# Cross attention and a max-out layer on one core: the state transposes go to the DMA queue, and GpSimd and VectorE work is reordered

## The chip, the cores and the metric

One core of one Trainium2 chip runs the whole kernel. The metric is the device time of one execution in microseconds; the time before is 148.46 us, the median of three runs (148.19 to 148.90).

## The reference

There are eight batches (B = 8) with eight heads (H = 8). Each head has 512 rows of x and 32 rows of state, 64 numbers wide.

```python
a = softmax(x @ state.T / 8)          # 512 x 32 for each batch and head
xread = a @ state                     # 512 x 64
a2 = softmax(state @ x.T / 8)         # 32 x 512
sread = a2 @ x                        # 32 x 64
attn = concatenate([xread, sread], axis=rows)      # 544 rows a batch
y = attn, heads laid side by side, (8*544) x 512
out = maximum(y @ w1, y @ w2) @ w_out              # 512 -> 1024 -> 512
```

## The kernel before

The kernel never forms xread. With wd = w1 - w2 it uses max(h1, h2) = relu(y wd) + y w2, so a batch's output is relu(A (S wd)) w_out + A (S (w2 w_out)), where A holds the softmax rows and S the state. For each batch it needs these pieces:

- `xt`, the batch's x transposed, and `sbd`, the transposed states in block form, for the scores. `scores_mm` and `scores_ev` make `e`, the exponentials. `reduce_pair` or `norm_sums` sum them and take the reciprocal (`er`), and `norm_mul` multiplies them to `a` (A, bf16).
- `aT`, `a` transposed: for batches 0 and 1 by TensorE (`at_mm`, eight transposes into two PSUM banks, copied out by `at_ev`), for later batches by a DMA (`at_dma`).
- `sw`, the state times wd, and the state times wwo = w2 w_out (`sw_mm`, `sw_two_mm`, `sw_h_mm`; copies `sw_ev`).
- first layer `l1_mm` (L426) with its relu `l1_ev` into `r`; second layer `l2_open` (L438) and `l2_f` (L442), copied to `ob` by `l2_out` and stored.
- `sread` for the state rows (`sread_mm`, `sread_norm`, `sread_tr_mm`), finished for all batches at the end (`moe_sread`).

The order of the instructions on every engine is the order in which the source issues them; no scheduler moves them. PSUM has two pools of four banks, `ps` and `pa` (tile names `ps` and `acc` in the profile). All loads, stores and DMA transposes go through SP's queue in source order, except for the first state load. An instruction that waits holds up everything behind it on its engine.

The opening stage, up to about 36 us, prepares the weights while batch 0 and then batch 1 run through it. Weights come in as f32 quarters of 512 KB and are cast to bf16 (`w2_cast`, `wo_cast`; the first quarter in halves: `w2_cast_h`, `w1_cast_h`, `wo_cast_h`); `w_sub` makes a quarter of wd; `w2_tr_mm` transposes a quarter of w2; `w_wo_mm` and `w_wo_h_mm` multiply it with w_out, and `w_wo_ev` adds up the rounds. `idle` issues matmuls on zeros while TensorE would wait. The states of batches 2 to 7 are loaded (`load_states`), cast on GpSimd (`states_cast`), transposed by TensorE (`states_mm`, line 157) into one bank, and copied to `sbd` by two engines (`states_ev`). For batch 2 on, x is cast by GpSimd in two halves (`cast_half`, `cast_x`) and transposed by a DMA (`xt_dma`); `cast_xo` makes another cast copy. A function `states_dma`, which transposes the states by a DMA into a buffer of the pool that holds the x casts, is in the source of the kernel before but not called.

After the opening, a loop over batches 1 to 7 issues one batch's second layer between the next batch's scores and first layer.

Of the kernel before, what the change touches and what calls it, by code (L numbers as in the profile page):

```python
# [15 lines left out]
def kernel(  # L16
# [9 lines left out]
    nc = tc.nc  # L26
    B, H, S, D = x.shape
    _, _, Ns, _ = state.shape
# [3 lines left out]
    NC = S // 128  # L32
# [14 lines left out]
    pa = ctx.enter_context(tc.tile_pool(name="pa", bufs=4, space=bass.MemoryType.PSUM))  # L47
    ctx.enter_context(tc.manual_schedule())

    def bank(dtype=F32, pool=None):  # L50
        n = 512 if dtype == F32 else 1024
        if pool is pa:
            return pa.tile([128, n], dtype, tag="acc", name="acc")
        return ps.tile([128, n], dtype, tag="ps", name="ps")

    def copy(eng, o, i):
        if eng == "A":
            nc.scalar.copy(o, i)  # L58
        elif eng == "V":
            nc.vector.tensor_copy(o, i)  # L60
        else:
            nc.gpsimd.tensor_copy(o, i)  # L62
# [20 lines left out]
    xf_t, st = {}, {}  # L83
# [40 lines left out]
    P = {}  # L124
# [26 lines left out]
    def states_cast(eng):  # L151
        copy(eng, sbr.rearrange("p m j d -> p j m d"), sfr.rearrange("p j (m d) -> p j m d", m=8))

    def states_mm(pool=None):
        p = P["st"] = bank(BF16, pool)
        for m in range(8):
            nc.tensor.transpose(p[:, m * 128:(m + 1) * 128], sbr[:, m].rearrange("p j d -> p (j d)"), ident)

    def states_dma():
        P["st"] = xio.tile([128, NC * 256], BF16, tag="xb", name="stt")  # L160
        nc.sync.dma_start_transpose(out=P["st"].rearrange("p (m r) -> p m r", m=8), in_=sbr.rearrange("p m j d -> p (m j d)"))

    def states_ev(j, eng):
        o = sbd[64 * j:64 * j + 64, 2:B, :, 32 * j:32 * j + 32].rearrange("p b k (l m) -> p (b k) l m", l=4)
        copy(eng, o, P["st"][64 * j:64 * j + 64, :].rearrange("p (m k l) -> p k l m", m=8, l=4)[:, 8:])


    def cast_half(b, g, eng):
        if b not in st:
            st[b] = dict(xb=xio.tile([128, NC, H * D], BF16, tag="xb", name="xb"))  # L170
        copy(eng, st[b]["xb"][:, :, 256 * g:256 * g + 256].rearrange("p c (i d) -> p i c d", i=4),
             xf_t[b][:, 4 * g:4 * g + 4, :].rearrange("p i (c d) -> p i c d", c=NC))
# [39 lines left out]
    def scores_pair_mm(b, k, pool):  # L212
        d = st[b]
        if "e" not in d:
            att_tiles(b)
        p = P["sc", k] = bank(F32, pool)
        for c in range(NC):
            nc.tensor.matmul(p[:, c * 64:c * 64 + 64], d["xt"][:, c, k, :], sbd[:, b, k, :],
                             start=(c == 0), stop=(c == NC - 1))

    def scores_pair_ev(b, k):
        nc.scalar.activation(out=st[b]["e"][:, :, :, k, :].rearrange("p g c n -> p c g n"),
                             in_=P["sc", k][:, 0:256].rearrange("p (c g n) -> p c g n", c=NC, g=2), func=ACTF.Exp, scale=scale)
# [6 lines left out]
    def xt_dma(b):  # L230
        d = st[b]
        d["xt"] = at.tile([128, NC, 4, 128], BF16, tag="xt", name="xt")
        nc.sync.dma_start_transpose(out=d["xt"].rearrange("p c k t -> p (c k) t"),
                                    in_=d["xb"].rearrange("p c m -> p (c m)"))
# [39 lines left out]
    def scores_ev(b, hh):  # L274
        ev = st[b]["e"].rearrange("p g c i n -> p (g c) i n")[:, :, 2 * hh:2 * hh + 2, :]
        nc.scalar.activation(out=ev.rearrange("p (g c) i n -> p g c (i n)", g=2),  # L276
                             in_=P["sc", hh].rearrange("p (c g m) -> p g c m", c=NC, g=2), func=ACTF.Exp, scale=scale)
# [5 lines left out]
    def norm_sums(b, hh, sums=True):  # L283
        d = st[b]
        if sums:
            ev = d["e"].rearrange("p g c i n -> p (g c) i n")[:, :, 2 * hh:2 * hh + 2, :]
            nc.vector.tensor_reduce(d["es"][:, hh], ev, axis=mybir.AxisListType.X, op=ALU.add)  # L287
        nc.vector.reciprocal(d["er"][:, hh], d["es"][:, hh])

    def norm_mul(b, hh, eng):  # L290
        d = st[b]
        ev = d["e"].rearrange("p g c i n -> p (g c) i n")[:, :, 2 * hh:2 * hh + 2, :]
        av = d["a"].rearrange("p g c i n -> p (g c) i n")[:, :, 2 * hh:2 * hh + 2, :]
        (nc.gpsimd if eng == "P" else nc.vector).tensor_mul(  # L294
            av, ev, d["er"][:, hh].unsqueeze(3).to_broadcast([128, 2 * NC, 2, Ns]))

    def norm(b, hh, eng, sums=True):
        norm_sums(b, hh, sums)
        norm_mul(b, hh, eng)
# [12 lines left out]
    def at_mm(b, g, pool=None):  # L312
        if b not in AT:
            AT[b] = keep.tile([128, 2, NC, 128], BF16, tag="at", name="aT")
        p = P["at", g] = bank(BF16, pool)
        for c in range(NC):
            nc.tensor.transpose(p[:, c * 128:(c + 1) * 128], st[b]["a"][:, g, c].rearrange("p i n -> p (i n)"), ident)

    def at_ev(b, g, eng):
        copy(eng, AT[b][:, g].rearrange("p c t -> p (c t)"), P["at", g][:, 0:512])  # L320
# [43 lines left out]
    def sw_ev(b, lo, hi, g, eng):  # L364
        copy(eng, SW[b][:, g, lo:hi], P["sw", b, lo][g][:, 0:hi - lo])
# [53 lines left out]
    R, OB, ACC = {}, {}, [None] * NC  # L419
# [16 lines left out]
    def l2_open(b, c, p, start, stop):  # L436
        for g in range(2):
            nc.tensor.matmul(p, AT[b][:, g, c, :], SW[b][:, g, FF:WC], start=(start and g == 0), stop=(stop and g == 1))  # L438

    def l2_f(b, c, p, fs, start, stop):  # L440
        for j, f in enumerate(fs):
            nc.tensor.matmul(p, R[b][:, f, c * 128:(c + 1) * 128], wo[:, f, :],  # L442
                             start=(start and j == 0), stop=(stop and j == len(fs) - 1))

    def l2_out(b, c, p, eng):
        if b not in OB:
            OB[b] = big.tile([128, NC, DM], F32, tag="ob", name="ob")
        copy(eng, OB[b][:, c, :], p)
# [62 lines left out]
    def w1_cast_h(j, eng):  # L511
        copy(eng, w1b[:, :, 128 * j:128 * j + 128], w1f[0][:, :, 128 * j:128 * j + 128])

    def wo_cast_h(j, eng):
        copy(eng, wo[:, j, :], wof[0][:, j, :])

    def w2_tr_h_mm(j, pool=None):
        p = P["w2h", j] = bank(BF16, pool)
        for i in range(4):
            nc.tensor.transpose(p[:, i * 128:(i + 1) * 128], w2b[0][:, i, j * 128:(j + 1) * 128], ident)  # L520

    def w2_tr_h_ev(j, eng):
        copy(eng, w2t[:, j].rearrange("p i t -> p (i t)"), P["w2h", j][:, 0:512])
# [15 lines left out]
    def w_sub(q, i0, i1, eng):  # L539
        (nc.gpsimd if eng == "P" else nc.vector).tensor_sub(  # L540
            wd[:, i0:i1, q * FQ:(q + 1) * FQ], w1f[q][:, i0:i1], w2f[q][:, i0:i1])
# [12 lines left out]
    def w_wo_h_mm(i, j, pool=None):  # L554
        if j == 0:
            P["wwo", 0, i] = bank(F32, pool)
        nc.tensor.matmul(P["wwo", 0, i], w2t[:, j, i, :], wo[:, j, :], start=(j == 0), stop=(j == 1))
# [16 lines left out]
    def l2_part(q, c):  # L574
        if ACC[c] is None:
            ACC[c] = bank(F32, pa)
        l2_f(0, c, ACC[c], (2 * q, 2 * q + 1), q == 0, False)
# [67 lines left out]
    xt_pair_ev(0, 3, "A")  # L645
    idle(1)
    scores_pair_mm(0, 2, None)
    wo_cast_h(0, "P")
    scores_pair_ev(0, 2)
    reduce_pair(0, 2)  # L650
    idle(5)
    scores_pair_mm(0, 3, pa)
    scores_pair_ev(0, 3)
    w2_tr_h_mm(0)
    w1_cast_h(1, "P")
    w1_cast_h(0, "A")
    idle(3)
    sread_mm(0, pa)
# [1 line left out]
    sw_h_mm(0, pa)  # L660
    reduce_pair(0, 3)
    norm_sums(0, 1, False)
    norm_mul(0, 1, "V")
    w2_tr_h_ev(0, "A")
    sw_ev(0, 0, 128, 1, "A")
    idle(4)
    w_wo_h_mm(1, 0)
    at_mm(0, 0, pa)
    sw_ev(0, 0, 128, 0, "A")
    at_mm(0, 1)  # L670
    w_sub(0, 0, 4, "P")
    w_wo_h_mm(3, 0)
    w2_cast_h(1, "A")
    at_ev(0, 1, "V")
    sw_h_mm(1, pa)
    sw_ev(0, 128, 256, 1, "V")
    wo_cast_h(1, "P")
    w2_tr_h_mm(1)
    at_ev(0, 0, "A")
    l1_mm(0, 0)  # L680
# [103 lines left out]
    scores_mm(1, 1)  # L784
    l2_part(2, 2)
    states_cast("P")
    scores_ev(1, 0)
    cast_half(2, 0, "P")
    scores_ev(1, 1)
# [3 lines left out]
    sw_ev(0, FF, WC, 0, "A")  # L793
    norm_sums(1, 0)
    norm_mul(1, 0, "P")
    l2_part(3, 2)
    l2_part(3, 1)
    l2_part(3, 3)
    sw_mm(1, FF, WC)
    norm_sums(1, 1)  # L800
    sw_ev(1, FF, WC, 0, "A")
    sread_mm(1)
    norm_mul(1, 1, "P")
    l2_open(0, 3, ACC[3], False, True)
    l2_open(0, 2, ACC[2], False, True)
    l2_out(0, 3, ACC[3], "A")
# [1 line left out]
    at_ev(1, 0, "A")  # L808
    sw_ev(1, FF, WC, 1, "V")
    at_mm(1, 1)  # L810
    cast_half(2, 1, "P")
    sread_norm(1)
    states_mm()
    states_ev(1, "A")
    at_ev(1, 1, "V")
    cast_xo(2)
    l2_out(0, 2, ACC[2], "V")
    l2_open(0, 0, ACC[0], False, True)
    l2_open(0, 1, ACC[1], False, True)
    states_ev(0, "V")  # L820
    l2_out(0, 1, ACC[1], "A")
    l2_out(0, 0, ACC[0], "V")
    l1_mm(1, 6, pa)
    cast_half(3, 1, "P")
    l1_ev(1, 6, "A")
# [4 lines left out]
    l1_mm(1, 7)  # L830
    l1_mm(1, 1, pa)
    l1_mm(1, 3, pa)
    xt_dma(2)
    l1_ev(1, 5, "A")
    l1_ev(1, 0, "V")
    l1_mm(1, 2)
# [13 lines left out]
    for b in range(1, B):  # L850
        n = b + 1
# [65 lines left out]
```

## Time and profile before

| | |
|---|---|
| median of the runs | 148.46 us |
| the profiled execution's own time | 148.07 us |
| its span, first to last instruction | 146.3 us |
| TensorE busy | 140.9 us, 96% of the span |
| VectorE, ScalarE, GpSimd busy | 83.8, 69.5, 59.3 us |
| bytes moved by DMA | 29.18 MB |
| granted TensorE clock | full throughout |

The profiled execution lies 1.77 us above its span (what comes before the first and after the last instruction) and 0.39 us below the median. In the profile, PE is a TensorE matmul or transpose and PEld its weight load, DVE is VectorE, ACT ScalarE, POOL GpSimd, SP the engine whose queue issues the DMAs. A row of a timeline gives start, time taken, engine, line, operation, output and input, count, and in brackets the idle time before it with what ended it.

### The profile page before, as it was taken

To read this page: it belongs to the slowest core of one execution; us is meant where nothing else is said; L and a number is where in the kernel's file an instruction comes from. 1 tells how busy PE (TensorE), PEld (TensorE's weight loads), DVE (VectorE), ACT (ScalarE), POOL (GpSimd) and SP (SyncE) were. 2 spreads that over 40 slices of the span, in tenths; PEclk is the share of its full clock that TensorE was granted. 3 is DMA by queue.
4 is the path that set the end of the run, shared out by engine and by line. 5 is a ranking of instruction groups with operands and counts; after the bars stand their busy time and mean duration, and the time that the engine had idled before them with its cause. 6 is when DMAs were issued, how large, how long until landed. Compare 5 with 4: busy or idle time off the path is not lost.

```text
span 146.3 us, 3237 instructions
## 1 busy us (share of the span) xinstructions
PE 140.9 (96%) x1314; PEld 71.5 (49%) x1314; DVE 83.8 (57%) x172; ACT 69.5 (47%) x135; POOL 59.3 (41%) x81
## 2 busy tenths in 40 slices
PE   6998999999999999999999999999999999999990
PEld 4764454364554445444544544454445344754460
DVE  3595695877874648464854675376557464621110
ACT  4387757686971456326450825271547135511110
POOL 2479435767948442925292347226500500000000
PEclk9999999999999999999999999999999999999999
DMA  3999999995459989496949685787306032402432
GB/s 126 308 321 351 356 362 362 361 350 165 93 104 338 211 286 283 81 270 246 242 85 286 251 184 109 250 297 138 72 36 251 8 73 121 166 4 72 143 121 94
DMA packets 36640, 29.18 MB, mean 199 GB/s; under 512 B 20241, under 2 KB 33809, under 8 KB 35729
## 3 DMA queue, kind: packets, MB, share of 16 engines
q1 hardware_dynamic: 36352, 28.91, 66.9%
q8 instruction: 10, 0.16, 0.4%
q10 hardware_dynamic: 272, 0.07, 0.2%
q14 instruction: 6, 0.04, 0.1%
HBM read 15.34 MB, written 8.91 MB: 166 GB/s over the span
## 4 chain that ended last, share of the span: by engine, by line
PE 91%; POOL 4%; DVE 2%; issue 0%; ACT 0%; POOLq 0%
PE acc L442 37%; PE ps L426 17%; PE acc L438 10%; PE ps L552 4%; PE acc L572 3%; PE ps L361 3%; PE ps L482 2%; PE acc L492 2%; PE ps L271 2%; POOL wd L540 2%; PE acc L328 1%; PE acc L466 1%; PE acc L490 1%; PE acc L426 1%; PE ps L533 1%; PE acc L361 1%
## 5 line engine op out<-in xcount | busy, mean ns | idle before, releaser
L442 PE MATMUL acc<-wo,r 128*128 128x512 bf16 x248 | 59.6, 379 | 0.0
L442 PEld LDWEIGHTS <-r 128*128 128x128 bf16 x248 | 23.8, 98 | 28.7 <-issue 0.6
L58 ACT COPY ob<-acc 128x512 f32<-128x512 f32 (+2 forms) x17 | 9.4, 554 | 48.8 <-PE acc L442 27.9
L426 PE MATMUL ps<-aT,sw 128*128 128x512 bf16 x118 | 27.9, 379 | 0.0
L294 POOL TENSOR_TENSOR a<-e,er 128x512 bf16<-128x512 bf16 x15 | 15.5, 1049 | 27.6 <-ACT e L276 20.3
L417 DVE TENSOR_SCALAR r<-ps 128x512 bf16<-128x512 f32 x26 | 18.0, 692 | 14.5 <-PE ps L426 14.4
L415 ACT ACTIVATE r<-ps 128x512 bf16<-128x512 f32 x33 | 19.7, 601 | 6.4 <-PE ps L426 5.7
L60 DVE COPY ob<-acc 128x512 f32<-128x512 f32 (+1 forms) x17 | 10.9, 644 | 16.3 <-PE acc L442 14.6
L426 PEld LDWEIGHTS <-sw 128*128 128x128 bf16 x128 | 12.2, 98 | 13.7
L62 POOL CAST xb<-xf 128x1024 bf16<-128x1024 f32 x12 | 12.4, 1040 | 15.1 <-DMA xf<-in_x_dram 15.1
L62 POOL CAST xo<-xf 128x512 bf16<-128x512 f32 x28 | 16.1, 615 | 5.8 <-DMA xf<-in_x_dram 5.4
L438 PE MATMUL acc<-sw,aT 128*128 128x512 bf16 x62 | 18.2, 380 | 0.0
L60 DVE CAST sw<-ps 128x512 bf16<-128x512 f32 x15 | 9.8, 687 | 12.0 <-PE ps L361 11.6
L58 ACT CAST sw<-ps 128x512 bf16<-128x512 f32 (+1 forms) x21 | 11.0, 573 | 2.9 <-PE ps L361 1.5
L287 DVE TENSOR_REDUCE es<-e 128x16 f32<-128x512 bf16 x14 | 9.2, 656 | 1.6 <-ACT e L276 1.6
L572 PE MATMUL acc<-wz 128*128 128x256 bf16 x38 | 7.9, 354 | 1.2 <-DVE ones L610 1.2
L276 ACT ACTIVATE e<-ps 128x512 bf16<-128x512 f32 x14 | 7.7, 597 | 0.8 <-PE ps L271 0.2
L438 PEld LDWEIGHTS <-aT 128*128 128x128 bf16 x62 | 5.0, 98 | 4.4
L552 PE MATMUL ps<-wo,w2t 128*128 128x512 bf16 x24 | 6.7, 380 | 0.0
L563 DVE TENSOR_TENSOR w2acc<-ps,w2acc 128x512 f32<-128x512 f32 x8 | 5.2, 686 | 1.7 <-PE ps L552 1.6
L572 PEld LDWEIGHTS <-wz 128*128 128x128 bf16 x38 | 4.3, 126 | 2.3 <-DVE ones L610 1.2
L540 POOL TENSOR_TENSOR wd<-w1f,w2f 128x1024 bf16<-128x1024 f32 x2 | 4.7, 2354 | 1.7 <-DMA w1f<-in_moe_w_dram 1.7
(109 smaller groups left out, 146.4 us busy)
## 6 DMA issues: line engine op xcount, KB each, us to landing
xf<-in_x_dram SPq DMA_DIRECT2D x14, 512.0 KB, 5.3
out_dram<-ob SPq DMA_DIRECT2D x7, 1024.0 KB, 4.2
w2f<-in_moe_w_dram SPq DMA_DIRECT2D x3, 512.0 KB, 8.1
w1f<-in_moe_w_dram SPq DMA_DIRECT2D x3, 512.0 KB, 9.1
wof<-in_moe_w_out_dram SPq DMA_DIRECT2D x3, 512.0 KB, 9.1
xf<-in_x_dram SPq DMA_DIRECT2D x4, 256.0 KB, 3.7
out_dram<-ob SPq DMA_DIRECT2D x3, 256.0 KB, 2.0
w2f<-in_moe_w_dram SPq DMA_DIRECT2D x2, 256.0 KB, 5.4
```

Of the source, the lines that this page charges most:

```text
L58: nc.scalar.copy(o, i)
L60: nc.vector.tensor_copy(o, i)
L62: nc.gpsimd.tensor_copy(o, i)
L287: nc.vector.tensor_reduce(d["es"][:, hh], ev, axis=mybir.AxisListType.X, op=ALU.add)
L294: (nc.gpsimd if eng == "P" else nc.vector).tensor_mul(av, ev, d["er"][:, hh].unsqueeze(3).to_broadcast([128, 2 * NC, 2, Ns]))
L415: nc.scalar.activation(out=o, in_=p, func=ACTF.Relu)
L417: nc.vector.tensor_scalar(o, p, scalar1=0.0, scalar2=None, op0=ALU.max)
L426: nc.tensor.matmul(p, SW[b][:, g, f * 128:(f + 1) * 128], AT[b][:, g].rearrange("p c t -> p (c t)"), start=(g == 0), stop=(g == 1))
L438: nc.tensor.matmul(p, AT[b][:, g, c, :], SW[b][:, g, FF:WC], start=(start and g == 0), stop=(stop and g == 1))
L442: nc.tensor.matmul(p, R[b][:, f, c * 128:(c + 1) * 128], wo[:, f, :], start=(start and j == 0), stop=(stop and j == len(fs) - 1))
L552: nc.tensor.matmul(p, w2t[:, f, i, :], wo[:, f, :], start=(f == fs[0]), stop=(f == fs[-1]))
L572: nc.tensor.matmul(idle_p[0][:, 0:cols], wz[:, 0:128], wz[:, 0:cols], start=True, stop=True)
```

## The change

The states of batches 2 to 7 are transposed by a DMA issued from SP (`states_dma`) in place of the eight TensorE transposes of `states_mm`, and the two `states_ev` copies then read SBUF instead of PSUM and stand a little later. The second half of batch 0's product `a` is made pair by pair: pair 2 by GpSimd, pair 3 by VectorE, instead of both by VectorE. GpSimd's first `wo_cast_h` and `w1_cast_h` come after that product, and its second `wo_cast_h` comes ahead of `w_sub(0)` instead of behind it. `at_mm(0, 0)` takes a bank of `ps` and `w_wo_h_mm(1, 0)` one of `pa`, and the latter is issued after the A transposes. For batch 1 the second product moves from GpSimd to VectorE; `cast_half(2, 1)` and `xt_dma(2)` come earlier, and `sread_norm(1)` comes behind `at_ev(1, 1)`.

```diff
+    def norm_mul_pair(b, k, eng):
+        d = st[b]
+        ev = d["e"].rearrange("p g c i n -> p (g c) i n")[:, :, k, :]
+        av = d["a"].rearrange("p g c i n -> p (g c) i n")[:, :, k, :]
+        (nc.gpsimd if eng == "P" else nc.vector).tensor_mul(
+            av, ev, d["er"][:, k // 2, :, k % 2].unsqueeze(2).to_broadcast([128, 2 * NC, Ns]))
...
     scores_pair_mm(0, 2, None)
-    wo_cast_h(0, "P")
     scores_pair_ev(0, 2)
...
     w2_tr_h_mm(0)
-    w1_cast_h(1, "P")
     w1_cast_h(0, "A")
...
     norm_sums(0, 1, False)
-    norm_mul(0, 1, "V")
+    norm_mul_pair(0, 2, "P")
+    norm_mul_pair(0, 3, "V")
+    wo_cast_h(0, "P")
+    w1_cast_h(1, "P")
     w2_tr_h_ev(0, "A")
     sw_ev(0, 0, 128, 1, "A")
     idle(4)
-    w_wo_h_mm(1, 0)
-    at_mm(0, 0, pa)
+    at_mm(0, 0)
     sw_ev(0, 0, 128, 0, "A")
     at_mm(0, 1)
+    w_wo_h_mm(1, 0, pa)
+    wo_cast_h(1, "P")
     w_sub(0, 0, 4, "P")
...
     sw_ev(0, 128, 256, 1, "V")
-    wo_cast_h(1, "P")
     w2_tr_h_mm(1)
...
     states_cast("P")
+    states_dma()
     scores_ev(1, 0)
...
     norm_mul(1, 0, "P")
+    cast_half(2, 1, "P")
     l2_part(3, 2)
...
     norm_sums(1, 1)
+    norm_mul(1, 1, "V")
     sw_ev(1, FF, WC, 0, "A")
     sread_mm(1)
-    norm_mul(1, 1, "P")
...
     at_mm(1, 1)
-    cast_half(2, 1, "P")
+    xt_dma(2)
+    at_ev(1, 1, "V")
     sread_norm(1)
-    states_mm()
-    states_ev(1, "A")
-    at_ev(1, 1, "V")
     cast_xo(2)
     l2_out(0, 2, ACC[2], "V")
     l2_open(0, 0, ACC[0], False, True)
     l2_open(0, 1, ACC[1], False, True)
+    l2_out(0, 1, ACC[1], "A")
+    states_ev(1, "A")
+    l2_out(0, 0, ACC[0], "V")
     states_ev(0, "V")
-    l2_out(0, 1, ACC[1], "A")
-    l2_out(0, 0, ACC[0], "V")
     l1_mm(1, 6, pa)
...
     l1_mm(1, 3, pa)
-    xt_dma(2)
     l1_ev(1, 5, "A")
```

## The prediction

> **What bounds the kernel now.** I read the page's chain of waits first, then the chain in order of time, then the waits and the timeline of the stretches that the change touches.
>
> ```profile
> PE 91%; POOL 4%; DVE 2%; issue 0%; ACT 0%; POOLq 0%
> ```
>
> ```profile
> 9.79 0.29 POOL wo L62
> 10.08 0.21 issue
> 10.29 1.08 POOL w1b L62
> 11.36 2.31 POOL wd L540
> 13.68 0.57 POOL wo L62
> 14.25 0.04 issue
> 14.29 0.38 PE ps L557
> ...
> 37.00 0.45 PE ps L317 x8
> 37.44 0.45 PE ps L157 x8
> 37.89 0.86 PE acc L438 x4
> ```
>
> The first fence is the page's shares, the second the chain in order of time (start, length, what). There are two regimes. From 8.7 to 14.3 us the chain runs through GpSimd: it ends in the cast of w_out's second eighth, behind the 2.31 us of `w_sub` (L540), and TensorE waits for it. From 16.07 us to 142.76 the chain has nothing but TensorE, so there only work taken off TensorE, or a new wait put before it, moves the end. The eight state transposes (L157) are 0.45 us of that part.
>
> Before trusting the early wait as a gain I looked at what comes due after it (timeline, 12 to 24 us, then waits, 13 to 19 us).
>
> ```profile
> 17.41 1.04 POOL L62 CAST wo<-wof 128x1024 bf16<-128x1024 f32 x1 [2.18 <-DMA wof<-in_moe_w_out_dram]
> 17.82 0.69 DVE L60 COPY w2t<-ps 128x1024 bf16<-128x1024 bf16 x1 [0.55 <-PE ps L533]
> 18.57 1.04 PE L552 MATMUL ps<-wo,w2t 128*128 128x512 bf16 x4
> ```
>
> ```profile
> PE ps L557 <- POOL wo L62: 0.6, 1, 0.6
> ```
>
> The matmuls L552 at 18.57 (`w_wo_mm(1, 1)`) need the second quarter of w_out, cast by GpSimd from 17.41 to 18.45. GpSimd had been idle 2.18 us for its load. That load is issued at 8.94 and lands 8.4 us later behind the other weights, with the DMA share above 1.0 in every stretch from 4 to 34 us. So 18.45 is fixed by bytes, and whatever TensorE gains before it is waited away there.
>
> **The early part.** Durations are rows of the timeline. The second product took VectorE 1.04 us (9.86 to 10.90) and `at_mm` started on it at 10.95. The halves cost about 0.53 on GpSimd (half of 1.05 in row L294) and 0.3 to 0.5 on VectorE, both from 9.82. The full product's start overlaps the cast 9.73 to 10.34, and 10.34 to 10.90 is 0.56; the GpSimd cast L62 behind it took 1.08 where its like takes 0.61. So the two engines seem to have taken turns, and I let the halves run one after the other: ready between 10.4 and 10.8, `at_mm` 0.1 to 0.5 us earlier. GpSimd then goes 10.7, first w_out cast 11.3, w1 cast 11.9, second w_out cast 12.5 (0.61 each), `w_sub` 14.85 (2.35). The w1 cast gates `sw_h_mm(1)`: 11.95 instead of 11.72, so the first-layer matmuls behind it are about 0.2 later. `w_wo_h_mm(3, 1)` needs the second w_out cast, now 12.5 instead of 14.24, so TensorE runs through: about 13.7 instead of 14.29. State batch 1 and its copy follow 0.6 earlier (second `sw_mm` group at 15.45 instead of 16.07), and wd's first quarter, 14.85, is still there before it. TensorE then arrives at L552 at about 17.95 and waits for 18.45. The smallest hand-over from GpSimd to TensorE in the chain is 0.05 (14.24 to 14.29), so L552 starts at 18.50: 0.07 us is all that remains of some 0.6. The same cover works the other way: the early part costs nothing until it is 0.07 later than before at L552. Next late would be the quarter casts that follow the loads; the w2 cast ends 20.04 where its transposes start at 20.74, the wd quarter of 24.76 has 0.7 too.
>
> `w_sub` ending 1.2 later holds SP's load of the last w2 quarter (issued at 13.71, when wd ended) and all loads behind it to about 14.9. Cover: the load ahead of it, issued at 10.28, lands 10.1 us later, so the DMA engines have work to 20.4. Cost nothing; without that cover 1.2 us at 22 us.
>
> At-transposes in other banks and the moved `w_wo_h_mm(1, 0)` have no wait of their own: the w_out cast is there at 11.3, TensorE leaves `at_mm` at about 11.2; 0.1 at most, inside the same cover.
>
> **The late part.** Taken off TensorE: 8 transposes, 0.45 us. The Trainium skill ("TensorE: Matmul & The Clock Gate", Part 4: PE-mode transpose) puts one such transpose at about 275 ns in a kernel; eight would be an estimated 2.2 us, and the whole change 2.3 us. The trace differs: each takes 219 ns but they start 56 ns apart, and the chain counts 0.45.
>
> Added: a DMA transpose on SP behind the state cast, which ends at 31.90 (30.86 + 1.04). It is 8 blocks, as the `aT` transposes are.
>
> ```profile
> xt<-xb SPq DMA_TRANSPOSE x6, 6.5
> aT<-a SPq DMA_TRANSPOSE x6, 3.1
> ```
>
> ```profile
> 34.00:35.00 1.00, 1.00 (x6) 0.39 (x4) 0.89 (x3) 1.00 (x2) 0.76 (x1) 1.00 0.59 179
> 35.00:36.00 1.00, 1.00 (x43) 0.46 (x42) 0.24 (x1) 0.34 (x2) 1.00 (x2) 1.00 0.13 40
> 36.00:37.00 1.00, 1.00 (x11) 0.53 (x8) 1.00 (x5) 0.71 (x2) 1.00 (x2) 1.00 0.02 5
> ```
>
> These are median times from issue to landing, and stretches of the busy table whose last two columns are the DMA share and GB/s. The x loads end between 35 and 37. If the transpose goes beside them it lands at 31.9 + 3.1 = 35.0; if it begins only when the last load has ended, at about 36.7 + 3.1 = 39.8. The longest `aT` took 4.2 (its tile's row), but fewer loads stood ahead of it; these loads are issued by 29.0, well before, so I lean to the late end and take 38. Who waits: on ScalarE `states_ev` (0.79 before, from PSUM) stands behind `l2_out` and would start at 38.85, so relus start at 39.5 instead of 39.28; the third of them frees the bank for the last sread transpose at 41.1, TensorE is there at 41.65. So the landing may be as late as 39.4 without cost, and each us beyond costs one. On VectorE the sum from 37.48 is 0.42 + 0.67 (`sread_norm`) + 0.68 + 0.67 + 0.95 (`states_ev`) + 2 x 0.69, less overlaps of about 0.08 each: 41.76 for the relu whose bank the second layer needs at 42.17. Slack 0.4. (`sread_norm`, moved into this stretch, gives its bank back at 38.5 instead of 37.04; the next user, `l1_mm(1, 0)`, comes at about 39.5.) `states_ev` reading SBUF is in no row; bounds 0.4 (VectorE's 512-element SBUF cast) and 0.95; I take 0.95, the same operation.
>
> "SBUF — State Buffer" (Who interferes with whom) of the Trainium skill says that a VectorE copy between SBUF operands can take both ports and that it and a GpSimd instruction then block each other whole. No row before shows this copy. By it `states_ev` would wait for a cast of up to 1.04, and 0.45 would shrink to nothing.
>
> `xt_dma(2)`: GpSimd loses a product (1.05), so its cast ends 36.3 instead of 37.27, or 36.9 if VectorE's product (0.6 to 1.04, from 34.95) holds it up. The transpose landed 4.5 after issue, at 41.8, for scores at 42.16. Now 40.8 to 41.4, or 42.5 if it queues behind the latest state transpose (39.8, and 2.7 us of transfer, which is the stretch 38.5 to 41.5 at a DMA share of 0.92), for scores at 41.7. I take 41.2: no wait. `at_mm(1)` at 36.84 has its product by 36.1 instead of 36.30, and the `sw` copy queued behind the product on VectorE starts at most 0.3 later than at 35.76, for a bank that is wanted at about 38.2.
>
> **Sum.** 0.45 + 0.07 = 0.52 us. The profiled execution would be 148.07 - 0.52 = 147.55; on the median, 148.46 - 0.52 = 147.94, which is 0.35% less. About 0.5%, 0.74 us, is what a measurement of this kernel can tell from no change, so this is a small gain inside "same".
>
> **The rivals.** (a) The gate at 18.45 does not hold: the early wait is paid in full, 0.6 + 0.45 = 1.05 us, 147.4. For it: 0.6 us of idle TensorE in plain sight. Against: the 2.18 us that GpSimd waited for that load. (b) The gain is given back: VectorE's `states_ev` is held up by a GpSimd cast, as the product at 9.86 was, here by up to 1.04; less the slack of 0.4 that is 0.6 of waiting, 148.5. For it: GpSimd casts without a pause there, from 38.8 to 40.8. Against: the hold-up needs VectorE to arrive early in a cast. (c) Slower: the state transpose lands late and ScalarE stands at `states_ev` with five relus and both score exponentials behind it. It decides from 39.4; a landing 9.3 us after issue, the median of the loads just before it, is 41.2: a stall of 1.8, less 0.52, so 149.7. Against: by then the queue is nearly empty.
>
> **How the numbers follow.** Forecast 0.6, (a) 0.12, (b) 0.18, (c) 0.1. The runs before spread 0.7 us, so of the forecast's 0.6 about 0.12 falls beyond 0.74 us. Faster 0.12 + 0.12 = 0.24, slower 0.1, same 0.66. The range goes from (a), 147.4, to a little above (b), 148.7, which is also the worst of the two open costs; it leaves out (c) and the tails.
>
> **What would show it.** Right: no L157 transposes on TensorE; `w_wo_h_mm(3, 1)` (L557 before) without its 0.6 wait; the quarter cast of w_out still at 17.4 behind its load, and a wait of TensorE of about half a us at `w_wo_mm(1, 1)`; the span 0.5 shorter from 38 us on, with the chain all TensorE. Wrong: `w_wo_mm(1, 1)` starting before 18.4 (a), or TensorE waiting between 38 and 43 us for a relu, `states_ev` or `xt` (b, c).

## The result, and the profile after

The changed kernel takes 148.13 us (median of 6 runs, 147.97 to 148.24), the kernel before 148.66 (6 runs on the same chip, 148.13 to 148.92): ratio 0.9969 [0.9946, 0.9992]. In two later sets, with more runs, the ratio was 0.998 [0.9962, 0.9998] and 0.9988 [0.9963, 1.0013]. So it is faster by 0.1 to 0.3%, inside what the forecast called no change (147.94, "same" at 0.66). Executions that lie 2.4 to 3.3 us above their kernel's median are left out of the medians from here on (of twelve, four in the kernel before with a late x load and two in the changed kernel with it; at most one elsewhere).

The profiled execution is no faster at all: 148.24 us with a span of 146.5, against 148.07 and 146.3 before. It is the place to read where the 0.45 us of the late part went. Line numbers behind line 296 are 7 higher than before. The page's shares of the chain:

```profile
PE 89%; DMA 3%; ACT 3%; issue 1%; SPq 1%; DVE 0%; POOL 0%; POOLq 0%
```

GpSimd's 4% is gone from this chain, but not by the reorder alone: the chain now comes from a late x load, and in the changed kernel's second profile, where x is early, GpSimd has 5%. Two shares are new: DMA 3%, which is one x load at the very start (the SPq 1% is the issue of the loads ahead of it), and ACT 3%, which the forecast had at nothing. The chain in order of time (start, length, what) puts ScalarE's share at 38.5 to 42.3 us:

```profile
37.19 0.45 PE ps L324 x8
37.63 0.88 PE acc L445 x4
...
38.53 0.45 ACT ob L58
38.98 0.16 issue
39.14 1.56 ACT sbd L58
...
40.72 1.58 ACT r L422 x3
...
42.34 0.22 PE acc L353
42.56 0.47 PE ps L271 x16
```

The eight state transposes between the A transposes (L324) and the second-layer matmuls (L445) are gone, and TensorE comes there 0.45 sooner after the A transposes. Then the chain leaves TensorE for ScalarE's half of the state copy, which is 1.56 long, and three relus behind it. The second sread transpose (L353) needs the bank that the third relu frees. The waits name the same pair:

```profile
PE acc L353 <- ACT r L422: 0.3, 1, 0.3
```

The timeline's rows of the two copies, before and then after (start, length, engine, line, operation):

```profile
37.93 0.79 ACT L58 COPY sbd<-ps 64x768 bf16<-64x768 bf16 x1
38.75 0.95 DVE L60 COPY sbd<-ps 64x768 bf16<-64x768 bf16 x1 [0.25 <-ACT sbd L58]
```

```profile
39.14 1.55 ACT L58 COPY sbd<-stt 64x768 bf16<-64x768 bf16 x1
39.79 1.28 DVE L60 COPY sbd<-stt 64x768 bf16<-64x768 bf16 x1
```

The same copy in the same order of elements takes ScalarE 1.55 from SBUF and 0.79 from PSUM. ScalarE also starts it 1.2 later, behind `l2_out`, so that its relus start at 40.72 instead of 39.28.

The early part, in the timeline of the changed kernel:

```profile
12.61 0.61 POOL L62 CAST wo<-wof 128x512 bf16<-128x512 f32 x1
...
17.13 1.36 POOL L62 CAST wo<-wof 128x1024 bf16<-128x1024 f32 x1 [0.61 <-DMA wof<-in_moe_w_out_dram]
18.76 1.04 PE L559 MATMUL ps<-wo,w2t 128*128 128x512 bf16 x4
```

The second w_out cast ends 1.0 earlier than before and no wait for it is left in the waits of 13 to 19 us, but `w_wo_mm(1, 1)` (L559, before L552) starts at 18.76 instead of 18.57. A pair of rows at the other end explains why it is not earlier. GpSimd's cast of batch 0's third x quarter, before and after:

```profile
5.80 0.61 POOL L62 CAST xo<-xf 128x512 bf16<-128x512 f32 x1 [4.34 <-DMA xf<-in_x_dram]
```

```profile
6.77 0.61 POOL L62 CAST xo<-xf 128x512 bf16<-128x512 f32 x1 [5.32 <-DMA xf<-in_x_dram]
```

The x load landed 1 us later in this execution. That is no part of the change, and all but 0.19 of it had been made good by L559. So the two profiled executions can't be compared by their spans: the shift has to be followed from mark to mark.

### The profile page after: what moved, and what is told of

Its sections match the earlier page's. It is cut to its first block, busy times and chain, and to the rows that moved or that the text cites. A ratio compares the mean times of both kernels' runs of the same rounds, so it can differ in the third digit from the quotient of the medians.

```text
span 146.5 us, 3225 instructions
## 1 busy us (share of the span) xinstructions
PE 140.5 (96%) x1306; PEld 70.9 (48%) x1306; DVE 84.2 (57%) x173; ACT 70.1 (48%) x135; POOL 59.9 (41%) x81
## 4 chain that ended last, share of the span: by engine, by line
PE 89%; DMA 3%; ACT 3%; issue 1%; SPq 1%; DVE 0%; POOL 0%; POOLq 0%
PE acc L449 37%; PE ps L433 16%; PE acc L445 10%; PE ps L559 4%; DMA xf<-in_x_dram 3%; PE ps L368 3%; PE ps L489 2%; PE acc L499 2%; PE ps L271 2%; PE acc L335 2%; PE acc L579 1%; PE acc L473 1%; PE acc L497 1%; ACT r L422 1%; ACT sbd L58 1%; PE ps L540 1%
## 5 line engine op out<-in xcount | busy, mean ns | idle before, releaser
L58 ACT COPY ob<-acc 128x512 f32<-128x512 f32 (+2 forms) x17 | 9.4, 554 | 49.1 <-PE acc L449 27.7
L294 POOL TENSOR_TENSOR a<-e,er 128x512 bf16<-128x512 bf16 x14 | 14.4, 1048 | 27.7 <-ACT e L276 20.2
L62 POOL CAST xb<-xf 128x1024 bf16<-128x1024 f32 x12 | 13.5, 1128 | 15.6 <-DMA xf<-in_x_dram 15.6
L445 PE MATMUL acc<-sw,aT 128*128 128x512 bf16 x62 | 18.2, 380 | 0.0
L58 ACT CAST sw<-ps 128x512 bf16<-128x512 f32 (+1 forms) x21 | 11.0, 574 | 2.9 <-PE ps L368 1.5
L445 PEld LDWEIGHTS <-aT 128*128 128x128 bf16 x62 | 5.0, 98 | 4.4
L559 PE MATMUL ps<-wo,w2t 128*128 128x512 bf16 x24 | 6.7, 380 | 0.0
L271 PEld LDWEIGHTS <-xt 128*128 128x128 bf16 x112 | 4.3, 98 | 2.1 <-issue 0.5
```

The lines of the kernel that those rows point to most:

```text
L294: (nc.gpsimd if eng == "P" else nc.vector).tensor_mul(av, ev, d["er"][:, hh].unsqueeze(3).to_broadcast([128, 2 * NC, 2, Ns]))
L559: nc.tensor.matmul(p, w2t[:, f, i, :], wo[:, f, :], start=(f == fs[0]), stop=(f == fs[-1]))
```

## The experiments

**Theory 1** is the forecast: the eight transposes give 0.45 in the late part, the copies from SBUF are covered, and the early part gives 0.1 at most because `w_wo_mm(1, 1)` waits for the second w_out quarter in any case. **Theory 2**, from the traces: the late 0.45 is given back by the long copy, and what the median gains comes from the early part, in those executions in which an x load lands late.

**Halves of the change.** The early part alone, with everything from `states_dma` on as before:

```diff
-    states_dma()
...
+    states_mm()
+    states_ev(1, "A")
...
```

> The kernel before with the early edits alone: products of pairs 2 and 3 on two engines, the order of GpSimd's casts, the banks of the A transposes. Theory 1 (as forecast): the second w_out quarter lands at about 17.3 us and gates TensorE, so the early edits pay at most 0.1 us: ratio 0.999 to 1.000. Theory 2 (from the trace after): an x load of batch 0 lands about 1 us late in some executions; the order before passes that on and the new order takes most of it up, while the late part gains nothing. Then nearly all of the measured 0.5 us is here: ratio about 0.997, and a smaller spread of the runs than before, by the highest coming down and not the lowest.

Measured: 148.05 (12 runs), before 148.40 (28 runs); 0.9986 [0.9963, 1.001]. The smaller spread that was expected did not come: 1.38 us for its 12 runs, and 1.38 for the 28 before. The late part alone, with the early order of the kernel before:

> The kernel before with the late edits alone: states transposed by DMA, second product of batch 1 on VectorE, earlier x cast and x transpose. Theory 1: 0.45 us off TensorE reach the end: ratio 0.997. Theory 2: ScalarE's state copy from SBUF takes about 1.55 us instead of 0.79 and the relus behind it hold TensorE for 0.4 to 0.5 us at the sread transposes: ratio 0.999 to 1.001, with the spread of the kernel before.

Measured: 148.63 (12 runs); 1.0009 [0.9988, 1.0031]. Neither interval excludes no change; the order is that of theory 2, with the gain in the early part and none in the late part. Its profile has the long copy (39.90, 1.55) and the wait of L353 for the relu again. Marks within one execution are sharper than medians. From batch 1's first A transpose to batch 2's first score matmul it is 5.32 us before and with the early part alone, 5.37 with the late part alone and 5.38 in the changed kernel.

The whole change with the states transposed on TensorE again (`states_mm` and copies from PSUM, where the kernel before has them), the rest of the late reorder kept:

> The changed kernel with the states transposed by TensorE again and copied from PSUM as before; all other edits stay. Theory 1: 0.45 us slower than the changed kernel, ratio to the kernel before about 1.000. Theory 2: same as the changed kernel within 0.1 us, ratio about 0.997, since the transposes that come back cost what the slow copy from SBUF cost.

Measured: 148.27 (12 runs); 0.9984 [0.9964, 1.0003]; the stretch is 5.32. So the DMA transpose with its copies and the TensorE transposes with theirs cost the same, to 0.06 us.

**Both copies on GpSimd**, ahead of its cast copy of batch 2:

```diff
+    states_ev(1, "P")
+    states_ev(0, "P")
     cast_xo(2)
...
-    states_ev(1, "A")
     l2_out(0, 0, ACC[0], "V")
-    states_ev(0, "V")
```

> The changed kernel with both state copies on GpSimd, ahead of its casts of batch 2, so that neither ScalarE nor VectorE makes one. Theory 1: the copies cost nothing where they were, so this is the same as the changed kernel: 0.997 against the kernel before. Theory 2: the 0.45 us of the state transposes come out at last: 0.45 us below the changed kernel, ratio about 0.994, and TensorE waits for no relu between 38 and 43 us. If GpSimd's copies take over 2 us each, the states come after 41.7 us and TensorE waits for them at the scores of batch 2.

Measured: 151.98 (6 runs); 1.0244 [1.0197, 1.029]. The sread transposes are early (41.63, none waiting for a relu), so ScalarE is free of its load; the kernel loses 4 us elsewhere. The state transpose landed at 38.97 here and GpSimd's two copies took 3.08 from 39.10, so that TensorE waited 0.33 for them at the scores of batch 2 (the stretch is 5.36), and GpSimd was 1.6 us behind at its next products (46.62 instead of 44.98). The transpose of batch 2's `a` is issued by SP at 49.45 instead of 47.06 and lands 5.96 later. TensorE then stands at the first-layer matmuls, says the table of waits:

```profile
PE ps L433 <- DMA aT<-a: 2.7, 1, 2.7
```

**ScalarE's copy alone on GpSimd**, between its casts for batches 2 and 3:

```diff
-    states_ev(1, "A")
...
     l1_mm(1, 6, pa)
+    states_ev(1, "P")
     cast_half(3, 1, "P")
```

> The changed kernel with ScalarE's half of the state copy (1.55 us at 39.14) put on GpSimd between its batch 2 and batch 3 casts, where it should run from about 39.4 to 40.9; VectorE's half stays. Theory 2 (the late gain is given back by ScalarE's slow copy, through the bank that its fourth relu holds up): ScalarE's relus begin at about 39.3 instead of 40.7, the second state transpose goes without its 0.3 wait, scores of batch 2 start some 0.4 us earlier after the A products than in the changed kernel (4.9 to 5.0 after at_mm of batch 1 instead of 5.38), and the median falls to about 147.7. Theory 1 (the copy is covered; the 0.45 is already in the time of the changed kernel): no change, 148.1. If GpSimd's later casts are late by the 1.5 us of the copy (with both halves on GpSimd they were late by about 3 and cost 4 us), 148.5 or more.

Measured: 148.84 (12 runs); 1.0026 [1.0005, 1.0046], slower and not the 147.7 expected. The stretch is 4.87: the 0.5 us came out. Half a us is lost at the very next step, and the chain of this kernel shows to whom:

```profile
39.63 1.20 DVE ob L60 x2
40.82 1.79 DVE sbd L60
42.61 1.79 DVE r L424 x3
44.41 0.26 DVE sread_t L60 x2
```

It is now VectorE throughout. Its half of the copy took 1.88 (row 40.74), as GpSimd's copy ran from 40.43 to 41.94. VectorE's copy ended 0.67 behind that, at 42.61; the two GpSimd casts that followed at 42.00 took 2.50, where a pair takes 2.02 alone. So each engine held up the other. VectorE's relus hold up the second-layer matmuls by 0.55, and a further 0.44 goes by 54 us, 0.3 of it where batch 2's first-layer matmuls wait for the transpose of a late `a`.

**The copy cut in two.** Batch 2's scores need only batch 2's sixth of the states. The other five sixths go to ScalarE behind batch 2's exponentials, where it stood idle for 3.1 us:

```diff
+    def states_ev(j, eng, b0=2, b1=B):
...
-    states_ev(1, "A")
+    states_ev(1, "A", 2, 3)
     l2_out(0, 0, ACC[0], "V")
-    states_ev(0, "V")
+    states_ev(0, "V", 2, 3)
...
                 scores(n, hh)
+            if b == 1:
+                states_ev(1, "A", 3)
+                states_ev(0, "A", 3)
```

> The changed kernel with the state copy cut in two: batch 2's sixth (64x128 for each half) stays where it was, on ScalarE and VectorE, and the other five batches' follow on ScalarE behind batch 2's two exponentials, where it stood idle for 3.1 us (two copies of about 1.3 us, 44.2 to 46.9). Theory 2 (the late gain is given back by the 1.55 and 1.28 us copies): each early copy takes 0.25 to 0.35 us, the stretch from batch 1's A transposes to batch 2's scores shrinks from 5.38 to 4.85 to 4.95 and nothing behind it is later, as GpSimd and VectorE have no new work beside each other; 147.65 to 147.8, 0.4 under the changed kernel and 0.7 to 0.8 under the kernel before. Theory 1 (the copies are covered): 148.15, as the changed kernel.

Measured: 147.53 (12 runs, 147.18 to 148.24), before 148.24 on that chip; 0.9946 [0.9919, 0.9972]. It beats both kernels. The early copies took 0.41 and 0.74, more than the 0.25 to 0.35 expected, and nothing waited for them. The stretch is 4.88, and the chain from 37 to 42.5 us has only TensorE in it:

```profile
37.08 0.45 PE ps L324 x8
37.53 0.86 PE acc L445 x4
...
41.41 0.43 PE ps L433 x2
41.85 0.11 PE acc L353 x2
41.96 0.47 PE ps L271 x16
```

From batch 2's first score matmul to the last matmul it is 100.31 us, as before (100.31) and in the changed kernel (100.32), so nothing is given back later. The same cut with the late part alone:

> The late edits alone (early part as in the kernel before), with the same cut of the state copy. Theory 2: the 0.45 of the eight transposes taken off TensorE comes out in full, so 148.0 where the late edits alone gave 148.63 and the kernel before 148.4 to 148.5; the early part still passes a late x load on, so it stays some 0.3 above the version that has both. Theory 1: no difference from the late edits alone, 148.6.

Measured: 147.83 (12 runs, 147.45 to 148.29); 0.9961 [0.9936, 0.9987]; the stretch is 4.88. The early part on top of it is worth the 0.30 to 147.53, though the runs of the two overlap. The changed kernel on that chip:

> The changed kernel as the measure of the other two on this chip: 148.15, 0.2 to 0.4 under the kernel before, by both theories. Its third profiled execution adds one more pair of numbers, start of GpSimd's x cast against start of the last early w_out product. From the seven profiles with the new order that product should start at the later of about 18.8 and 12.0 behind the cast's start; from the three with the old order at the later of about 18.6 and 12.5 behind it.

Measured: 148.25 (12 runs); 0.9988 [0.9963, 1.0013]. By the medians it is no faster than the kernel before on that chip (148.24, 29 runs).

**Which of the two copies.** ScalarE's half cut, VectorE's left whole:

> The changed kernel with only ScalarE's half of the state copy cut in two (batch 2 in place, the other five batches behind batch 2's exponentials); VectorE's half stays whole, 1.28 us, of which about 0.62 is waiting for the GpSimd cast that runs when it arrives. This tells the two copies apart. If ScalarE's copy alone gave the 0.45 back: from batch 1's A transposes to batch 2's scores 4.88 instead of 5.38, the first second-layer matmul of the next group within 0.15 us of its place in the version with both halves cut (5.34 behind the A transposes), and 147.5 to 147.7. If VectorE's hold-up by GpSimd (the mechanism of rival b) took part of it: that matmul waits for VectorE's second relu, at about 5.3 to 5.9 behind the A transposes, and the time lies between, at 147.8 to 148.2. Theory 1 (both copies covered): 148.2, as the changed kernel.

Measured: 147.71 (7 runs, 147.12 to 147.91), before 148.76 on that chip; 0.9928 [0.9899, 0.9958], no different from both halves cut; the stretch is 4.94 by the timeline and 4.88 in the chain. VectorE's copy still takes 1.29 in it and nothing waits for that. So it was ScalarE's copy that gave the 0.45 back. One row shows how near another wait lies:

```profile
39.11 0.41 ACT L58 COPY sbd<-stt 64x128 bf16<-64x128 bf16 x1 [0.47 <-DMA stt<-sbr]
```

The state transpose landed at 39.1 in this execution, against 37.2 in the changed kernel's first profile. ScalarE stood 0.47 idle for it.

**The late x load.** The load of the third first-layer weight quarter goes ahead of batch 0's third and fourth x quarters, in the kernel before and in the changed one, so that these x quarters land late every time:

```diff
+    load_h(0, 2)
     load_x(0, 4, 2)
     load_x(0, 4, 3)
-    load_h(0, 2)
```

> The kernel before, with the third first-layer weight quarter's load issued ahead of batch 0's third and fourth x quarters, so that these land some 0.8 us later in every execution. Theory 2 (the old early order lets a late x load through to TensorE): the last early w_out product starts at about 19.3 to 19.5 instead of 18.57, and the time is 0.6 to 0.9 us above the kernel before, about 149.3. Theory 1 (that product is released by the second w_out quarter's cast, whatever comes before): within 0.2 us of the kernel before.

Measured: 149.00 (8 runs), before 148.46 (34 runs) on that chip: 0.54 more, where 0.6 to 0.9 was expected.

> The changed kernel with the same swap of loads. Theory 2: the reordered early part takes the lateness up; the last early w_out product starts at 18.7 to 18.9, and the time is at most 0.2 us above the changed kernel, about 148.2; so against the kernel before with the same swap it is some 0.7 us faster. Theory 1: both swapped kernels stand as the unswapped ones do, 0.1 from the early part alone.

Measured: 148.58 (10 runs), 0.40 above the changed kernel's 148.18 (11 runs):

> The changed kernel once more, on the chip of the other three, as their measure: 148.1, and 0.2 to 0.5 us under the kernel before. Both theories agree here; what it adds is the third x quarter's landing in a second profiled execution: if it lands near 5.7 there, the 6.65 of the first belongs to the execution and not to the kernel.

The expectation for the changed kernel, 0.2 at most, missed, and so did the 0.7 between the two swapped kernels, which is 0.42. The swap is no clean test of the early part. It moved the x quarter further than planned and not by the same amount (cast at 7.10 before, 7.46 after), and the kernel before lost time at a second place as well: the scores of batch 2 waited there for the transpose of x, so that the stretch is 5.55 instead of 5.32 (waits of 36 to 46 us):

```profile
PEld L271 <- DMA xt<-xb: 0.2, 1, 0.2
```

More shows when all profiles are put side by side. Start of GpSimd's x cast, end of the second w_out quarter's cast, start of `w_wo_mm(1, 1)`, from the timelines:

```
early order  kernel            x cast   w_out cast ends   w_wo_mm(1,1)
old          before             5.80         18.45           18.57
old          late half, cut     6.75         18.85           19.25
old          late half alone    7.00         19.12           19.52
old          before, x late     7.10         19.20           19.61
new          after, second time 5.66         18.86           18.91
new          copies on GpSimd   5.80         18.56           18.62
new          on TensorE again   5.86         18.70           18.76
new          both halves cut    5.87         18.62           18.67
new          one half cut       6.19         18.25           18.30
new          after              6.77         18.49           18.76
new          early half alone   6.83         18.66           18.82
new          after, third time  6.89         18.62           18.88
new          after, x late      7.46         19.19           19.46
new          one copy on GpSimd 7.72         19.44           19.71
```

Where x is early, the product starts 0.12 behind the w_out cast in the one profile of the old order and 0.05 to 0.06 behind it in the five of the new, where TensorE waits 0.2 to 0.5 for that cast (here with the states on TensorE again):

```profile
PE ps L559 <- POOL wo L62: 0.5, 1, 0.5
```

The cast's end varies too, from 18.25 to 18.86 among these. Where x is late, the product starts 12.50 to 12.52 us behind the x cast with the old order and 11.99 to 12.00 with the new one. The new order thus saves 0.5 us on the way from x, and that counts as soon as x is more than 0.3 late in the old order. The chain of the late half alone shows the path: it runs through VectorE's copy of the transposed w2, not through the w_out cast.

```profile
18.77 0.70 DVE w2t L60
19.47 0.05 issue
19.52 0.60 PE ps L559 x2
```

One subtraction ties these starts to the time. A profiled execution's own time less the start of this product is 129.46 to 129.52 us in eight profiles: the kernel before, each half alone, the states on TensorE again, the changed kernel three times and with a late x. It is 128.97 to 129.05 in the three versions with the copy cut, and 129.74 in the kernel before with a late x, which has the wait for x's transpose. So the late part as it was made moves the time by nothing, the cut takes off 0.5, and whatever else differs between these executions lies ahead of the product.

Of the twelve profiled executions with the loads in their usual order six had the x cast at 6.7 or later, so an estimate of what the early part is worth on average is half of 0.5. The medians lie near it: 0.35 (early half alone), 0.30 (the two cut versions), 0.28 and none for the changed kernel in its two later sets. None of these is far from noise by itself. The spread of the runs settles nothing: 0.65 us for 11 runs of the changed kernel and 1.55 for 34 of the kernel before, but 1.38 for 12 of the early half alone.

## Why the prediction was right, and which steps failed

The time and the class were right, the place was not: of the 0.52 forecast, 0.45 was to come from the late part, which gives nothing, and 0.07 from the early part, which gives all. That the two errors nearly cancel is luck. One of the forecast's own signs of being wrong, TensorE waiting for a relu between 38 and 43 us, came up in the trace (0.34 us), through the length of ScalarE's copy, which no rival named.

- **TensorE freed of 0.45 us: right.** The first-layer matmuls follow the A transposes by 1.31 instead of 1.75.
- **`states_ev` reading SBUF: the step that failed.** The prediction bounded it by 0.4 and 0.95 and took 0.95. It is 1.55 on ScalarE, 0.6 above the upper bound. Both bounds were VectorE rows, and the copy that mattered is ScalarE's; the prediction gave that half 0.79, its time from PSUM. With it the relus start at 40.72 where the forecast had 39.5 (0.19 of that is the later `w_wo_mm(1, 1)` of this execution). The forecast's slack, a third relu done at 41.1 for a TensorE that comes at 41.65, turns into the observed wait: the relu ends at 42.30. The "SBUF — State Buffer" page of the Trainium skill (Door 1: The DMA port swizzle, on SBUF "cachelines") says that a read which goes to another 16-byte line with each element pays for it. This copy reads that way, and ScalarE's row agrees. VectorE's does not: its half, read in the same order, takes 0.66 by itself (next point), less than its 0.95 from PSUM. A ScalarE cast that reads SBUF element after element had taken 0.63 for 512 elements (row L58 xo<-xf of the kernel before, at 29.53). No run here changed the order alone, so it is not shown that the order is what makes SBUF slow for ScalarE.
- **Rival (b), VectorE held up by a GpSimd cast: its mechanism is there, its price is not.** VectorE's copy began at 39.79 and ended 0.66 behind the end of the GpSimd cast that ran when it arrived (39.37 + 1.04 = 40.41). The pair of casts took longer by 0.60:

```profile
39.37 2.62 POOL L62 CAST xb<-xf 128x1024 bf16<-128x1024 f32 x2
```

  Two such casts take 2.02 in the kernel with both copies on GpSimd (row 44.63). So the copy is 0.66 by itself and waits 0.62, as the page's section on who interferes with whom has it. VectorE's slack absorbed that, which the version with ScalarE's half alone cut shows. With 0.6 more, in the version with ScalarE's copy on GpSimd, it decided.
- **The state transpose's landing: right, and a near miss.** Forecast 38, between 35.0 and 39.8, free until 39.4; it landed at 37.22, but in five of the ten profiles that have it at 38.96 to 39.25. The latest is the changed kernel's second, where ScalarE begins its copy at 39.28. Rival (c) needed 41.2.
- **`xt(2)`: right.** It landed at about 41.4 for 41.2 (issued at 36.95, 4.4 to its landing), no wait.
- **The gate at `w_wo_mm(1, 1)`: right where x is early, and wrong in not asking how often.** The half us that the forecast saw waited away is the 0.5 of the table. It was dismissed on the ground of one execution, whose own margin was 0.26 (5.80 + 12.51 = 18.31, against 18.57); x lands about 1 us later in every second execution. The times before already spread 0.7 us, and the constant 129.5 shows that such a spread belongs to the part ahead of this product, where it should have been looked for. Rival (a) foresaw that the early wait can be worth about half a us; it is so in half of the executions, and not because the gate fails but because x comes later.
- **Pair products one after the other: right.** VectorE's half took 0.42 (10.64) and GpSimd's 0.79 (10.75, against the forecast's 0.53 alone), and `at_mm` follows the reciprocals by 0.99 instead of 1.13. SP's delayed w2 load landed at 21.60, no later than before (21.83).

## What to carry to other kernels

When work is moved from TensorE to a transfer, price the copy behind it on each engine that makes it, from where it now reads and in its order of elements; a row of another engine is no bound. If that copy is too long, cut it by who needs it first: here a sixth was wanted at once and the rest 14 us later. A step that only one path gates today is worth what it saves in the executions where another path is last, so look at the spread of the times, and at several executions, before calling it free.

## What the runs showed of the hardware

- ScalarE's reordering copy of 64x768 bf16 takes 1.55 us from SBUF and 0.79 from PSUM; by size from SBUF it is 0.41 for 128 elements and 1.31 for 640, which is 1.76 ns an element and 0.18 fixed. For the same copy from SBUF VectorE needs 0.66 when it is not held up (what is left of its 1.28 and 1.88 once the GpSimd instruction has ended), and GpSimd 1.50.
- A VectorE copy between SBUF operands and a GpSimd cast or copy hold each other up. VectorE, coming second, ended 0.66 and 0.67 behind the GpSimd instruction for 768 elements, and its 128 elements took 0.74 behind a running cast; a pair of GpSimd casts behind the copy took 2.62 and 2.50 instead of 2.02.
- The same x load, issued at the same time, lands about 1 us later in six of twelve executions (its cast starts at 5.66 to 6.19, or at 6.75 to 7.72); in the changed kernel's trace one of its 16 parts was 1.3 us behind the others.
